# A retention layer and two dense layers in one program: the opening written as a table of single-engine steps

## The chip, the core and the metric

The kernel runs on one core of a Trainium2 chip. The metric is the time of one execution in device microseconds; the time of a version is the median of its runs. TensorE (PE in the views) multiplies matrices, with its weight loads shown apart as PEld; VectorE is DVE, ScalarE is ACT, GpSimd is POOL, and SyncE (SP) issues most of the transfers.

## What is computed

```python
# q, k, v: (2, 8, 768, 64); w_in: (512, 2048), w_out: (2048, 512), twice
gamma = 1.0 - 2.0 ** (-5.0 - arange(8))
for t in range(768):
    state = gamma * state + outer(k[t], v[t])     # per batch and head
    y[t] = q[t] @ state / sqrt(64)
x = y as (1536 tokens, 512)
h = x @ w_in1;  x = where(h > 0, h, exp(min(h, 0)) - 1) @ w_out1
h = x @ w_in2;  x = (max(h, 0) + log1p(exp(-abs(h)))) @ w_out2
```

q, k and v are float32. The four weights arrive as 8-byte numbers, from which the kernel rebuilds a float32 on the chip.

## The kernel before

**Retention.** The 1536 tokens are twelve tiles of 128, six for each batch entry. For tile j, q and k are transposed on TensorE (`ret_transpose`, L194); the transposed q is evacuated from PSUM by DVE, which multiplies it with the table gq of decays (L209), and the transposed k by ACT (L207). `ret_scores` (L236) multiplies the two and DVE applies the causal mask (L248). `ret_out` (L252) multiplies the state (where there is one) and the masked scores with the tokens' values; the result is a column block of the activations x, kept as a rounded high part xh (ACT, L272) and a low part xl (DVE, L273). `ret_state` (L218) carries the state to the next tile, `ret_wide` spreads it on POOL (L216), and `ret_prep` decays v on POOL (L192).

**The dense layers.** Four tiles make a block of 512 tokens; there are three blocks. A unit u is one of two layers, one of three blocks and one of sixteen slices of 128 hidden features, 96 units in all. `hidden(u)` (L297) is twelve matmuls of 128x512: the slice's high and low weights against xh and xl, three products by four parts of the depth. `act(u)` applies the activation, `act_split` splits its result into gh and gl (L326, L327), `project(u)` (L347) is twelve matmuls into four accumulators, and `finish` writes a finished block.

**Weights.** A weight slice arrives in a raw buffer (five of them, `load_w`, L129). `conv_w` rebuilds it: two operations on ACT (L143, L144), then two on DVE (L145, L146). `split_w` makes the high part wh on ACT (L157) and the low part wl on DVE (L158). The order of the slices is in `wq`; the next one is loaded when a buffer has been converted. From block 0 of the first layer 32 slices are converted, and 32 more for the second layer in block 2.

**What sets the order.** The schedule is manual: each engine takes its instructions in the order in which the program issues them, with semaphores between engines, and the order is that of the calls. The opening is written out (L393 to L425): `next_load(5)`, then `load_tile(4)`, then the four tiles with scores, output of the tile before, transposes of the next, state. From unit 0 on the loop at L438 issues for every u the split of u+3, the splits for u+1, `hidden(u+2)`, one conversion, one retention job of tiles 4 to 11 (transposes, scores, or output with state, L370), `project(u)`, `act(u+2)` and one or two conversions more. All loads of tiles and weights are on SP's queue, in this order; a load into a buffer still in use holds the queue. PSUM has eight banks: before unit 0 the retention rotates over seven, then over r0 and r1, while hidden uses h0 and h1 and project a0 to a3. `keep_clock(7)` (L107) runs seven matmuls on zeros ahead of the first transpose.

```python
    for s in range(TPB):
        ret_scores(s)
        ...
        if s:
            ret_out(s - 1)
        if s + 1 < TPB:
            ret_transpose(s + 1)
        ret_state(s)
```

Of the kernel before, what the change touches and what calls it, by code (L numbers as in the profile page):

```python
# [23 lines left out]
def tile_retention_elu_softplus(
# [43 lines left out]
    def load_tile(j):  # L68
        b, c = divmod(j, CPB)
        r = []  # L70
        for n, (src, nm) in enumerate(((q, "q"), (k, "k"), (v, "v"))):
            if j == 0 and n == 2:
                nc.sync.dma_start(out=gq, in_=decay_q)
            t = early[n][:, j] if j < TPB else rp.tile([P, H, D], F32, tag=nm, name=nm)
            nc.sync.dma_start(out=t, in_=src[b, :, c * P:(c + 1) * P, :].rearrange("h s d -> s h d"))
            r.append(t)
        qkv[j] = r
# [71 lines left out]
    free = {(0, f, o) for f in range(NF) for o in range(2)}  # L149

    def split_w(u, o):
        _, _, f = units[u]
        a = wf[f][o]
        sh = [P, DM] if o else [P, KK, P]
        h = wsp.tile(sh, F32R, tag=f"wh{o}", name="wh")
        l = wsp.tile(sh, F32R, tag=f"wl{o}", name="wl")
        nc.scalar.activation(out=h, in_=a, func=AF.Copy)  # L157
        nc.vector.tensor_tensor(out=l, in0=a, in1=h.bitcast(F32), op=ALU.subtract)  # L158
        ws[u, o] = (h, l)
        if units[u][:2] == (0, NB - 1):  # L160
            free.add((1, f, o))
# [334 lines left out]
```

## Time and profile before

| | |
|---|---|
| runs, us | 598.36, 598.55, 596.74 (median 598.36) |
| the profiled execution, us | 598.43 |
| its span, us | 596.7 |
| PE busy | 584.9 us, 98% |
| DVE busy | 463.9 us, 78% |
| ACT busy | 415.3 us, 70% |
| POOL busy | 24.9 us, 4% |
| mean granted clock of TensorE | 0.992 |

The span runs from the first to the last instruction of the profiled execution; its time has some two microseconds more around that. A granted clock of 1.00 is 2.4 GHz, 0.50 is 1.2 GHz. PE's busy share says little of how well it is used, since matmuls overlap; where it is idle, in what stretch and for whom, is read from the stretches, the timeline and the chain of waits.

### The profile page before, as it was taken

The page shows a single profiled execution, that of the slowest core. Times are in us where ns is not written, and L with a number is a line of the kernel's source. Part 1 is how long each engine was busy: PE and PEld are TensorE (multiplying, and loading weights), DVE is VectorE, ACT ScalarE, POOL GpSimd, SP SyncE. Part 2 cuts the span into 40 slices and gives each one's busy share as a digit, 9 for nine tenths or more (in the row PEclk, how much of TensorE's full clock was granted, in tenths as well). Part 3 has the DMA queues.
Part 4 walks back from the last instruction along what each step waited for, and adds up shares of the span by engine and source line. Part 5 has one row for each costly group of instructions (what it writes and reads, how often), then busy time and mean ns, then how long its engine had stood idle before and what let it go on. Part 6 is the DMA issues. An engine that isn't in the chain of part 4 may idle for free.

```text
span 596.7 us, 8178 instructions
## 1 busy us (share of the span) xinstructions
PE 584.9 (98%) x3031; PEld 482.0 (81%) x3031; DVE 463.9 (78%) x741; ACT 415.3 (70%) x699; POOL 24.9 (4%) x42
## 2 busy tenths in 40 slices
PE   8898999999999999999999999999999999999997
PEld 5776888888888888888888888888888888888885
DVE  3889999965655455898898999877877787878774
ACT  2499788844544465898898967776777667766763
POOL 3300200111011000000000000000000000000000
PEclk8998999999999999999999999999999999999999
DMA  9986776851010000355464000000100000100001
GB/s 200 285 238 211 196 209 197 211 127 35 18 36 2 1 0 8 99 177 164 156 206 145 1 1 1 1 0 1 71 1 1 0 1 0 71 1 2 0 1 71
DMA packets 61000, 46.94 MB, mean 79 GB/s; under 512 B 38816, under 2 KB 55200, under 8 KB 60960
## 3 DMA queue, kind: packets, MB, share of 16 engines
q1 hardware_dynamic: 60672, 46.14, 27.5%
q8 instruction: 24, 0.39, 0.3%
q10 hardware_dynamic: 288, 0.27, 0.1%
q14 instruction: 16, 0.13, 0.1%
HBM read 43.26 MB, written 3.15 MB: 78 GB/s over the span
## 4 chain that ended last, share of the span: by engine, by line
PE 95%; DVE 2%; ACT 1%; DMA 1%; issue 1%; SPq 0%; DVEq 0%; ACTq 0%
PE h L297 42%; PE a L347 37%; PE r L347 7%; PE r L241 2%; PE r L267 1%; PE r L200 1%; PE r L261 1%; DMA gq<-decay_q 1%; DVE cl L145 1%; PE r L225 0%; PE a L200 0%; PE a L241 0%; DVE wi L146 0%; PE h L241 0%; DVE wo L146 0%
## 5 line engine op out<-in xcount | busy, mean ns | idle before, releaser
L297 PE MATMUL h<-xh,wh 128*128 128x512 f32 x384 | 103.0, 390 | 1.8 <-ACT wh L157 1.0
L297 PE MATMUL h<-xh,wl 128*128 128x512 f32 x384 | 102.7, 389 | 0.0
L297 PE MATMUL h<-xl,wh 128*128 128x512 f32 x384 | 102.7, 389 | 0.0
L297 PEld LDWEIGHTS h<-xh,wh 128*128 128x128 f32 x384 | 71.8, 188 | 17.7 <-ACT wh L157 2.0
L297 PEld LDWEIGHTS h<-xh,wl 128*128 128x128 f32 x384 | 72.1, 188 | 15.0
L297 PEld LDWEIGHTS h<-xl,wh 128*128 128x128 f32 x384 | 72.1, 188 | 15.0
L157 ACT ACTIVATE wh<-wo 128x512 fp32r<-128x512 f32 x96 | 60.4, 629 | 34.0 <-PE a L347 30.5
L158 DVE TENSOR_TENSOR wl<-wo,wh 128x512 fp32r<-128x512 f32 x96 | 67.3, 701 | 15.3 <-ACT wh L157 15.2
L158 DVE TENSOR_TENSOR wl<-wi,wh 128x512 fp32r<-128x512 f32 x96 | 65.7, 685 | 0.1
L157 ACT ACTIVATE wh<-wi 128x512 fp32r<-128x512 f32 x96 | 59.5, 619 | 1.6 <-DVE wi L146 1.5
L347 PE MATMUL a<-gh,wh 128*128 128x512 f32 x192 | 57.8, 408 | 0.0
L347 PE MATMUL a<-gh,wl 128*128 128x512 f32 x192 | 54.4, 390 | 0.0
L347 PE MATMUL a<-gl,wh 128*128 128x512 f32 x192 | 54.3, 389 | 0.0
L145 DVE SCALAR_TENSOR_TENSOR cl<-cm,cl 128x512 int32<-128x512 int32 x64 | 46.0, 719 | 10.2 <-ACT cl L144 10.0
L326 ACT ACTIVATE gh<-w 128x512 fp32r<-128x512 f32 x48 | 30.4, 633 | 33.1 <-DVE w L318 33.1
L312 ACT ACTIVATE e<-h 128x512 f32<-128x512 f32 x48 | 28.6, 597 | 32.0 <-PE h L297 32.0
L315 DVE TENSOR_SCALAR w<-e 128x512 f32<-128x512 f32 x48 | 20.5, 426 | 36.9 <-ACT e L313 36.7
L144 ACT ACTIVATE cl<-raw,half 128x512 int32<-128x512 uint32 x64 | 48.0, 750 | 0.0
L307 DVE SCALAR_TENSOR_TENSOR e<-e,h 128x512 f32<-128x512 f32 x48 | 32.8, 683 | 16.2 <-ACT e L306 15.9
L347 PEld LDWEIGHTS a<-gh,wl 128*128 128x128 f32 x192 | 36.2, 188 | 7.8
L143 ACT ACTIVATE cm<-raw 128x512 f32<-128x512 f32 x64 | 42.2, 659 | 0.0
L347 PEld LDWEIGHTS a<-gl,wh 128*128 128x128 f32 x192 | 36.0, 188 | 7.6
(114 smaller groups left out, 904.0 us busy)
## 6 DMA issues: line engine op xcount, KB each, us to landing
raw<-moe_w_in SPq DMA_DIRECT2D x32, 512.0 KB, 4.0
raw<-moe_w_out SPq DMA_DIRECT2D x32, 512.0 KB, 3.4
out_dram<-o SPq DMA_DIRECT2D x11, 256.0 KB, 2.1
q<-q SPq DMA_DIRECT2D x8, 256.0 KB, 4.5
k<-k SPq DMA_DIRECT2D x8, 256.0 KB, 5.0
v<-v SPq DMA_DIRECT2D x8, 256.0 KB, 5.4
xl<-q SPq DMA_DIRECT2D x4, 256.0 KB, 5.2
xh<-k SPq DMA_DIRECT2D x4, 256.0 KB, 5.2
```

Source lines behind the costliest of these rows:

```text
L143: nc.scalar.activation(out=m, in_=hi.bitcast(F32), func=AF.Copy, scale=2.0 ** -112)
L144: nc.scalar.activation(out=l, in_=lo.bitcast(U32), func=AF.Relu, scale=2.0 ** -29, bias=half)
L145: nc.vector.scalar_tensor_tensor(out=l, in0=m.bitcast(I32), scalar=3, in1=l, op0=ALU.logical_shift_left, op1=ALU.bitwise_or)
L157: nc.scalar.activation(out=h, in_=a, func=AF.Copy)
L158: nc.vector.tensor_tensor(out=l, in0=a, in1=h.bitcast(F32), op=ALU.subtract)
L241: nc.tensor.matmul(bs[i][:, pr * P:(pr + 1) * P], kT[i * D:(i + 1) * D, pr, :], qT[i * D:(i + 1) * D, pr, :], start=(pr == 0), stop=(pr == ...
L297: nc.tensor.matmul(b, w[:, kk, :], x[:, kk, :], start=(n == 0), stop=(n == len(seq) - 1))
L307: nc.vector.scalar_tensor_tensor(out=e, in0=e, scalar=-1.0, in1=h, op0=ALU.add, op1=ALU.max)
L312: nc.scalar.activation(out=e, in_=h, func=AF.Abs)
L315: nc.vector.tensor_scalar(out=w, in0=e, scalar1=1.0, scalar2=-1.0, op0=ALU.add, op1=ALU.add)
L326: nc.scalar.activation(out=gh, in_=g, func=AF.Copy)
L347: nc.tensor.matmul(acc[i], st[:, i * P:(i + 1) * P], mv, start=(f == 0 and p == 0), stop=(f == NF - 1 and p == 2))
```

## The change

The program's calls are cut into steps that each concern one engine (and SP for loads), a dictionary gives each a short name, and the program is now a list of names with a number, `name.j`. Of the names: `Lq Lk Lv Lg Lw` load q, k, v of a tile, gq, and entry j of the weight list; `dq` and `dv` decay q and v; `Tq Tk` transpose on TensorE and `tq tk` evacuate; `S` scores and `m` masks; `O` outputs, `xh xl` their parts; `ST st` the state, `sp` its spreading; `ca cb` the halves of a conversion on ACT and DVE; `ih il oh ol` the splits of w_in and w_out; `H` hidden, `aa ab` the activation's parts, `gh gl` its split, `R` project, `F` finish; `kc` clock-keeping matmuls.

`regular()` generates a list in the manner of the old program. The 244 steps of the table `OPENING`, up to the sixth projection, are issued first, in the table's order; the rest of the generated list follows. Tiles 0 and 1 (those with a `dq` step) have q multiplied by its decay in place, on DVE, ahead of the transpose, and their evacuation is a copy; the table of decays grows from 12 to 20 columns for that. `keep_clock` is called for five matmuls more. `project` opens the accumulators at the first unit of a block that is issued (`fresh`), which in the table is unit 1. In the generated list a conversion's ACT half comes ahead of its DVE half with other steps between.

```diff
+OPENING = """
+Lq.0 Lk.1 Lk.0 Lq.1 dq.0 Lv.0 Tq.0 kc.3 Lk.2 Lq.2 Tk.0 kc.2 Lv.1 Tk.1 dq.1 tk.1 Lg.0 tq.0 Tq.1 Lv.2 tk.0 dv.0 tq.1 S.0
+Lk.3 ST.0 Lq.3 m.0 Lv.3 Tq.2 Tk.2 Lk.4 S.1 tk.2 dv.1 Lw.0 Lw.1 tq.2 Lw.2 ST.1 st.0 Lq.4 O.0 m.1 dv.2 Lw.3 S.2 Lq.5
...
-    def conv_w(layer, f, o):
-        if (layer, f, o) not in raws:
+    def conv_a(i):
+        if i not in raws:
...
+        nc.scalar.activation(out=m, in_=r[:, :, :, 1].bitcast(F32), func=AF.Copy, scale=2.0 ** -112)
+        nc.scalar.activation(out=l, in_=r[:, :, :, 0].bitcast(U32), func=AF.Relu, scale=2.0 ** -29, bias=half)
+        parts[i] = (m, l)
+
+    def conv_b(i):
...
+        m, l = parts.pop(i)
...
         nc.vector.scalar_tensor_tensor(out=l, in0=m.bitcast(I32), scalar=3, in1=l, op0=ALU.logical_shift_left, op1=ALU.bitwise_or)
...
+    def decay_query(j):
+        nc.vector.tensor_tensor(out=qkv[0, j], in0=qkv[0, j], in1=gt, op=ALU.mult)
...
+        if n:
+            nc.scalar.activation(out=tf, in_=b, func=AF.Copy)
+        elif j in plain:
+            nc.vector.tensor_copy(tf, b)
+        else:
+            nc.vector.tensor_tensor(out=tf, in0=b, in1=gq, op=ALU.mult)
...
-        if f == 0:
+        fresh = (layer, blk) not in opened
+        if fresh:
+            opened.add((layer, blk))
...
-    for u in range(NU):
-        layer, blk, f = units[u]
-        if u + LOOK + 1 < NU:
-            split_w(u + LOOK + 1, 0)
...
+        for u in range(NU):
+            cb()
+            if u + 3 < NU:
+                add("ih il", u + 3)
...
+            ca()
+            if u + 1 < NU:
+                add("oh ol gh gl", u + 1)
...
+            if u + 2 < NU:
+                add("H", u + 2)
+            cb()
+            if jobs:
+                names, j = jobs.pop(0)
...
+    opening = OPENING.split()
+    plain = {int(t[3:]) for t in opening if t[:3] == "dq."}
+    seen = set(opening)
+    rest = regular()
...
+    for t in opening + [t for t in rest if t not in seen]:
+        name, j = t.split(".")
+        steps[name](int(j))
```

**SP's queue at the start.** The early q, k and v lie in the tiles named xl_88, xh_89 and xl_90; raw is a weight's buffer. Before:

```order
L75 DMA xl_88<-q 128x8x64
L75 DMA xh_89<-k 128x8x64
L73 DMA gq<-decay_q 128x512
L75 DMA xl_90<-v 128x8x64
L75 DMA xl_88<-q 128x8x64
L75 DMA xh_89<-k 128x8x64
L75 DMA xl_90<-v 128x8x64
L75 DMA xl_88<-q 128x8x64
L75 DMA xh_89<-k 128x8x64
L75 DMA xl_90<-v 128x8x64
L75 DMA xl_88<-q 128x8x64
L75 DMA xh_89<-k 128x8x64
```

Now:

```order
L85 DMA xl_88<-q 128x8x64
L85 DMA xh_89<-k 128x8x64 x2
L85 DMA xl_88<-q 128x8x64
L85 DMA xl_90<-v 128x8x64
L85 DMA xh_89<-k 128x8x64
L85 DMA xl_88<-q 128x8x64
L85 DMA xl_90<-v 128x8x64
L414 DMA gq<-decay_q 128x512
L85 DMA xl_90<-v 128x8x64
L85 DMA xh_89<-k 128x8x64
L85 DMA xl_88<-q 128x8x64
L85 DMA xl_90<-v 128x8x64
```

k of tile 1 and k of tile 0 (in this order, one row for both) stand second and third, gq has gone from the third place to the ninth, behind v of tile 1, and v of tile 0 behind q of tile 1.

**TensorE around the first hidden matmuls.** The rows at the shape 128x128 and 64x128 are retention (L261, L267 outputs; then L295, L301 outputs, L222 transposes, L273 scores). Before, from the output of tile 3 to unit 2:

```order
L261 MATMUL a_409<-xh_91,wide_159 128x128 x4
L267 MATMUL a_409<-A,xl_90 64x128 x8
L297 MATMUL h_434<-xh_258,wh 128x512 x4
L297 MATMUL h_434<-xh_258,wl 128x512 x4
L297 MATMUL h_434<-xl_259,wh 128x512 x4
L297 MATMUL h_463<-xh_258,wh 128x512 x4
L297 MATMUL h_463<-xl_259,wh 128x512 x4
L297 MATMUL h_463<-xh_258,wl 128x512 x4
L297 MATMUL h_524<-xh_258,wh 128x512 x4
L297 MATMUL h_524<-xl_259,wh 128x512 x4
L297 MATMUL h_524<-xh_258,wl 128x512 x4
```

Now, over the same stretch up to the output of tile 4; of the eight score rows of tile 4 the first two are shown, and unit 1's three rows are left out:

```order
L295 MATMUL a_403<-xh_91,wide_146 128x128 x4
L301 MATMUL a_403<-A,xl_90 64x128 x8
L222 MATMUL a_425<-ident,k 128x128 x4
L222 MATMUL a_432<-ident,q 128x128 x4
L329 MATMUL h_448<-xh_293,wh 128x512 x4
L329 MATMUL h_448<-xh_293,wl 128x512 x4
L329 MATMUL h_448<-xl_294,wh 128x512 x4
L273 MATMUL r_475<-qT,kT 128x128
L273 MATMUL r_476<-qT,kT 128x128
L222 MATMUL r_516<-ident,q 128x128 x4
L295 MATMUL r_526<-qT,wide_145 128x128 x4
L301 MATMUL r_526<-A,v 64x128 x8
```

Tile 4's transposes stand ahead of unit 0, its scores behind unit 0, and the query transposes of tile 5 and tile 4's output behind unit 1, all ahead of unit 2; before, the hidden matmuls of units 0, 1 and 2 followed one another.

**DVE around tile 4's query.** cl and wi or wo are the two operations of a conversion, wl and gl low parts, qT the evacuation of a transposed query, L283 (L248 before) a mask. Before, the twelve rows up to tile 4's query:

```order
L146 SCALAR_TENSOR_TENSOR wi_134<-raw,cl 128x512
L307 SCALAR_TENSOR_TENSOR e<-e,h_524 128x512
L145 SCALAR_TENSOR_TENSOR cl<-cm,cl 128x512
L146 SCALAR_TENSOR_TENSOR wo_131<-raw,cl 128x512
L145 SCALAR_TENSOR_TENSOR cl<-cm,cl 128x512
L146 SCALAR_TENSOR_TENSOR wi_136<-raw,cl 128x512
L158 TENSOR_TENSOR wl<-wi_134,wh 128x512
L158 TENSOR_TENSOR wl<-wo_131,wh 128x512
L327 TENSOR_TENSOR gl<-e,gh 128x512
L145 SCALAR_TENSOR_TENSOR cl<-cm,cl 128x512
L146 SCALAR_TENSOR_TENSOR wo_133<-raw,cl 128x512
L209 TENSOR_TENSOR qT<-r_614,gq 128x512
```

Now, from the first conversion to the first mask of tile 4:

```order
L165 SCALAR_TENSOR_TENSOR cl<-cm,cl 128x512
L166 SCALAR_TENSOR_TENSOR wi_113<-raw,cl 128x512
L165 SCALAR_TENSOR_TENSOR cl<-cm,cl 128x512
L166 SCALAR_TENSOR_TENSOR wi_115<-raw,cl 128x512
L312 TENSOR_TENSOR xl_294<-h_378,xh_293 128x4x128
L179 TENSOR_TENSOR wl<-wi_113,wh 128x512
L312 TENSOR_TENSOR xl_294<-a_403,xh_293 128x4x128
L237 TENSOR_TENSOR qT<-a_432,gq 128x512
L179 TENSOR_TENSOR wl<-wi_115,wh 128x512
L165 SCALAR_TENSOR_TENSOR cl<-cm,cl 128x512
L166 SCALAR_TENSOR_TENSOR wi_117<-raw,cl 128x512
L283 TENSOR_TENSOR A<-r_475,mask 128x512
```

The evacuation of tile 4's query stands behind two conversions, two tiles' low parts and unit 0's; before, ten conversions went ahead of it.

## Rows read from the trace of the kernel before

**Rows 1.** The page, part 4: the chain that ended last, shares by engine.
```profile
PE 95%; DVE 2%; ACT 1%; DMA 1%; issue 1%; SPq 0%; DVEq 0%; ACTq 0%
```

**Rows 2.** Stretches, us: each engine's busy time, granted clock, DMA share, GB/s.
```profile
0.00:28.00 28.00, 23.48 (x256) 18.12 (x257) 15.53 (x27) 9.18 (x14) 9.66 (x22) 0.94 1.11 243
28.00:57.00 29.00, 26.00 (x120) 20.73 (x120) 26.55 (x43) 26.81 (x47) 1.34 (x2) 0.94 0.79 229
57.00:120.00 63.00, 63.00 (x390) 51.99 (x389) 59.41 (x94) 52.23 (x92) 5.04 (x7) 1.00 0.73 204
```

**Rows 3.** Timeline of TensorE, opening: start us, us, instruction, idle before and releaser.
```profile
1.26 3.00 PE L107 MATMUL wb<-warm 128*128 128x512 bf16 x7 [1.26 <-DVE warm L102]
4.14 0.63 PE L200 MATMUL h<-ident,xl 128*128 128x128 f32 x4
...
6.97 1.75 PE L241 MATMUL a<-qT,kT 64*128 64x128 f32 x16 [1.06 <-DVE qT L209]
...
27.73 1.20 PE L297 MATMUL h<-xh,wh 128*128 128x512 f32 x4 [0.70 <-ACT xh L272]
...
34.48 1.17 PE L297 MATMUL h<-xh,wh 128*128 128x512 f32 x4 [0.99 <-ACT wh L157]
...
51.57 1.96 PE L241 MATMUL r<-qT,kT 64*128 64x128 f32 x16 [1.87 <-DVE qT L209]
53.46 1.95 PE L347 MATMUL a<-gh,wh 128*128 128x512 f32 x4
55.26 1.07 PE L347 MATMUL a<-gh,wl 128*128 128x512 f32 x4
...
57.07 1.07 PE L297 MATMUL h<-xh,wh 128*128 128x512 f32 x4
```

**Rows 4.** The chain that ended last in order of time: start us, us, work.
```profile
1.93 4.11 DMA gq<-decay_q
...
16.96 1.09 PE h L261 x8
18.05 1.02 PE h L267 x16
19.07 1.02 PE a L200 x8
20.10 0.64 PE a L225 x16
...
71.63 2.72 PE h L297 x12
74.35 1.09 PE r L241 x16
...
214.30 2.72 PE a L347 x12
```

**Rows 5.** DMA issues: line's tile, queue, operation, count, KB each, median us to landing.
```profile
xl<-q SPq DMA_DIRECT2D x4, 256.0 KB, 5.2
...
dec<-decay ACTq DMA_DIRECT2D x1, 6.0 KB, 2.6
```

**Rows 6.** Timeline, opening, of SP's queue and of POOL.
```profile
5.81 0.94 SPq L75 DMA_DIRECT2D xl<-v  x1
...
7.37 1.05 POOL L192 TENSOR_TENSOR xl<-xl,dec 128x512 f32<-128x512 f32 x1 [4.78 <-DMA xl<-v]
...
22.89 1.04 POOL L192 TENSOR_TENSOR xl<-xl,dec 128x512 f32<-128x512 f32 x1
```

**Rows 7.** Timeline of DVE, conversions and splits.
```profile
23.55 0.93 DVE L145 SCALAR_TENSOR_TENSOR cl<-cm,cl 128x512 int32<-128x512 int32 x1
...
58.19 0.68 DVE L145 SCALAR_TENSOR_TENSOR cl<-cm,cl 128x512 int32<-128x512 int32 x1
...
59.52 0.69 DVE L158 TENSOR_TENSOR wl<-wi,wh 128x512 fp32r<-128x512 f32 x1
60.12 0.69 DVE L158 TENSOR_TENSOR wl<-wo,wh 128x512 fp32r<-128x512 f32 x1
```

More of the change, by code (lines that the diff above doesn't have):

```diff
@@ L66, in tile_retention_elu_softplus, with load @@
     qkv = {}
-    def load_tile(j):
+    def load(n, j):
         b, c = divmod(j, CPB)
[L70 to L77, printed above, removed]
+        src, nm = ((q, "q"), (k, "k"), (v, "v"))[n]
+        t = early[n][:, j] if j < TPB else rp.tile([P, H, D], F32, tag=nm, name=nm)
+        nc.sync.dma_start(out=t, in_=src[b, :, c * P:(c + 1) * P, :].rearrange("h s d -> s h d"))
+        qkv[n, j] = t
     early = [xpool.tile([P, TPB, H, D], F32, tag=t, name=t) for t in ("xl2", "xh2", "xl1")]
     early_t = xpool.tile([P, 4, HP, P], F32, tag="xh1", name="xh1")
-    dec = const.tile([P, H + HP], F32, name="dec")
+    dec = const.tile([P, 2 * H + HP], F32, name="dec")
     gq = const.tile([P, HP * P], F32, name="gq")
     nc.scalar.dma_start(out=dec, in_=decay)
-    for j in range(TPB):
-        load_tile(j)
     gv = dec[:, 0:H].unsqueeze(2).to_broadcast([P, H, D])
+    gt = dec[:, H + HP:].unsqueeze(2).to_broadcast([P, H, D])
     gs = dec[:, H:H + HP].unsqueeze(2).to_broadcast([P, HP, D])
@@ L148, in tile_retention_elu_softplus, with split_h, split_l @@
     ws = {}
-    free = {(0, f, o) for f in range(NF) for o in range(2)}
-    def split_w(u, o):
+    def split_h(o, u):
         _, _, f = units[u]
[L153 to L161, printed above, removed]
+        h = wsp.tile([P, DM] if o else [P, KK, P], F32R, tag=f"wh{o}", name="wh")
+        nc.scalar.activation(out=h, in_=wf[f][o], func=AF.Copy)
+        ws[u, o] = [h]
+    def split_l(o, u):
+        _, _, f = units[u]
+        l = wsp.tile([P, DM] if o else [P, KK, P], F32R, tag=f"wl{o}", name="wl")
+        nc.vector.tensor_tensor(out=l, in0=wf[f][o], in1=ws[u, o][0].bitcast(F32), op=ALU.subtract)
+        ws[u, o].append(l)
     slots = {}
@@ L287, in tile_retention_elu_softplus @@
     acc = {}
+    opened = set()
     def hidden(u):
@@ L314, in act, with act_b @@
             nc.scalar.activation(out=l, in_=e, func=AF.Ln, bias=one)
+            acts[u] = [e, l]
+    def act_b(u):
+        h = hb.pop(u)
+        e = acts[u][0]
+        if units[u][0] == 0:
+            nc.vector.scalar_tensor_tensor(out=e, in0=e, scalar=-1.0, in1=h, op0=ALU.add, op1=ALU.max)
+        else:
+            l = acts[u][1]
+            w = rp.tile([P, TB], F32, tag="qT", name="w")
             nc.vector.tensor_scalar(out=w, in0=e, scalar1=1.0, scalar2=-1.0, op0=ALU.add, op1=ALU.add)
@@ L346, in project @@
             st, mv = passes[p]
-            nc.tensor.matmul(acc[i], st[:, i * P:(i + 1) * P], mv, start=(f == 0 and p == 0), stop=(f == NF - 1 and p == 2))
+            nc.tensor.matmul(acc[i], st[:, i * P:(i + 1) * P], mv, start=(fresh and p == 0), stop=(f == NF - 1 and p == 2))
     def finish(u):
@@ L381, in next_load @@
-    def next_load(n):
-        for _ in range(n):
-            x = next(lw, None)
-            if x:
-                load_w(*x)
-    def next_conv(n):
-        for _ in range(n):
-            if cv and cv[0] in free:
-                conv_w(*cv.pop(0))
-                next_load(1)
-    next_load(5)
-    load_tile(4)
-    cv = list(wq)
-    ret_transpose(0)
-    ret_prep(0)
-    for s in range(TPB):
-        ret_scores(s)
-        if s == TPB - 1:
-            next_conv(1)
-        if s:
-            ret_out(s - 1)
-        if s + 1 < TPB:
-            ret_transpose(s + 1)
-        ret_state(s)
-        ret_wide(s + 1)
-        ret_prep(s + 1)
```

345 lines of the change are left out of this document (212 added, 133 removed).

## The prediction

> **What bounds the kernel now.** I read the page first: TensorE is on the chain that ended last for 95% of the span [rows 1], so only time that TensorE loses can be won. The stretches [rows 2] tell where it loses any: it is busy 63.00 of 63.00 us from 57 to 120 us (and goes on so to the last matmuls), but 23.48 of 28.00 before 28 us, and 26.00 of 29.00 from 28 to 57 us. The same rows show VectorE (DVE) at 26.55 of 29.00 and ScalarE (ACT) at 26.81 of 29.00 in the second stretch: there the weights' conversion and splitting fills both, and TensorE waits for them. In the third stretch DVE has 59.41 of 63.00, so it keeps up, barely.
>
> TensorE's own rows [rows 3] show the losses singly: 1.06 us for the first decayed query (whose multiplication waits for the table gq), 0.70 for the last tokens, 0.99 for the third split weight, 1.87 for tile 4's query. The last is the dearest, because the clock falls with it: tile 4's scores take 1.96 us and the first quarter of the next projection 1.95, where the same work takes 1.09 [rows 4] and, in that projection's next row, 1.07 [rows 3]. The first scores also ran slowly: 1.75 us.
>
> **What TensorE loses before.** T, S, O and ST are a tile's transposes, scores, outputs and state; H and R a unit's hidden and projection matmuls. At full clock they take 1.02 (T), 1.09 (S), 1.09 + 1.02 (O; 1.02 alone for tile 0, which has no state), 0.64 (ST), 2.72 (H) and 2.72 (R) [rows 4]. From the first transpose at 4.14 to the start of H.5 at 57.07 [rows 3] TensorE does T.0 to T.4 (5.10), S.0 to S.4 (5.45), O.0 to O.3 (1.02 + 3 x 2.11 = 7.35), ST.0 to ST.3 (2.56), H.0 to H.4 (13.60) and R.0 to R.2 (8.16): 42.2 us of work in 52.9. Lost: 10.7 us.
>
> **The change, part by part.**
>
> *The first loads.* On SP's queue k of tile 1 now stands second, k of tile 0 third, q of tile 1 fourth, q of tile 2 seventh, gq ninth. By place: the third issue of before (gq) landed 4.11 us after 1.93 [rows 4], so at 6.0; the fourth (v of tile 0) was in use at 7.37 [rows 6]. So k of tile 0 lands at 6.0 and q of tile 1 by 7.4. Later ones land 5.2 us after issue [rows 5]: q of tile 2 in the place issued at 5.81 [rows 6], at 11.0.
>
> *Query decay of tiles 0 and 1 ahead of the transpose (dq).* gq is no longer needed first; instead DVE multiplies q in place before T. That needs the table dec, which landed 2.6 us after its issue in the first microsecond [rows 5], and q of tile 0, on hand by 4.14. No such multiplication stands on DVE's rows; the nearest, a tensor-tensor with both inputs in SBUF, takes 0.69 [rows 7], the far end is POOL's product of the same shape with dec, 1.05 [rows 6]. I take 0.69, of the same engine: T of q.0 starts at 4.85 instead of 4.14, 0.71 lost (1.07 at the far end). For tile 1 it ends at 7.37 + 0.69 = 8.06; then tile 0's transposed query is evacuated, until 8.75 (a copy now, which I cost like a split, 0.69). S.0 starts at 8.9, where it started at 6.97. Both T.0 and T.1 are done by then: the 4.05 us from 4.85 hold 2.04 of work, 2.0 lost. The five added clock-keeping matmuls lie in these waits (for k.0 and q.1) and cost nothing; without that cover they would cost 5 x 3.00/7 = 2.1 [rows 3]. Whether S.0 still runs slowly (1.75 for 1.09) the rows leave open: between 0 and 0.66 lost. I take 0.66, since gaps remain ahead of it.
>
> *Tiles 1 to 3.* ST.0 ends by 11.2, about when q of tile 2 lands; I take 0.45 lost for a late q here or at tile 3. gq, two places on, is issued near 8 and lands near 13, and is first needed for S.2, which now comes behind S.1, ST.1 and O.0, at 15. The other waits of before are covered, since a tile's transposes stand well ahead of its scores. Lost in all: 0.71 + 2.0 + 0.66 + 0.45 = 3.8.
>
> *Tile 4 moved up.* T.4 fills the time in which H.0 waited 0.70 for tokens; S.4 stands between H.0 and H.1, O.4 before H.2, T.5 and ST.4 around H.2 and H.3: work that came later stands where the 0.99 was. Tile 4's query is evacuated on DVE ahead of the third conversion, so the 1.87 and the slow 1.7 behind it have no cause left. On SP, k.4 goes ahead of the first weight, which comes a place (some 0.9 us, as the 0.94 of [rows 6]) later; ACT is not free for it before tile 1's tokens, near 20. v.4 goes behind weight load 4, which waits until the first conversion frees its buffer: issued near 25, landed by 31, decayed on POOL by 32; O.4 comes at 34.4.
>
> *Conversions in halves.* The instructions are the same, ACT's half sooner. DVE is what can fail. A conversion takes 1.33 there, a split 0.61, start to start [rows 7]. With H.0 at 27.3 by the sum so far, DVE starts the first conversion at 23.4, behind tile 3's masks. Up to the low split of unit 3 it does six conversions (8.0), 0.5 extra for two beside POOL, eleven operations of 0.61 (6.7) and a short wait for S.4: done at 39.0, where H.3 wants it at 41. The low split of unit 4 follows at 49.4 (H.4 wants it at 50.3), gl of unit 1 comes at 42.7 (R.1 wants it at 43.5), gl of unit 3 at 55 (R.3 wants it at 56.9). DVE holds with 0.9 us to spare at the tightest.
>
> The 0.5 stands for this: the conversion's first operation took 0.93 instead of 0.68 while POOL ran its product [rows 7]. The Trainium skill's "SBUF — State Buffer", section "SBUF: two separate sides", has the port pair of these two engines as an exclusive lock: the loser waits out the other's whole instruction. By that rule each of the two meetings could cost up to POOL's 1.04, 2.1 for the 0.5; the 0.9 to spare would be gone and TensorE lose 0.7, 592.2 for the sum below. The row shows a quarter of that, so the sum keeps the row.
>
> *Later.* From unit 12 on as many conversions stand ahead of each H as before, and tiles 5 to 11 come three units sooner on an engine that is never idle there: no cost. Done before H.5 beyond the old list are R.3, T.5, S.5, O.4 and ST.4: 2.72 + 1.02 + 1.09 + 2.11 + 0.64 = 7.6. H.5 then starts at 4.14 + 3.8 + 42.2 + 7.6 = 57.7, 0.7 late with 7.6 done: a gain of 6.9, which is also 10.7 - 3.8. The profiled execution took 598.43 (span 596.7), 0.07 over the median of 598.36. **598.4 - 6.9 = 591.5 us.** If the clock holds and q.2 lands in time, 2.7 are lost and it is 590.4; if q.1 is on hand with k.0 at 6.0 too, S.0 comes 1.4 sooner: 589.0.
>
> **Rivals.** *DVE comes late.* Between 28 and 57 us it idled 29.00 - 26.55 = 2.45 us before. If that idling stays, R.1 or H.4 waits 2.45 - 0.9 = 1.6, and such a wait cost a fallen clock of 0.87 + 0.88 = 1.7 last time: 3.3 given back, 594.8. For it: its 94% up to 120 us. Against: ACT's halves, which it depends on, now lead. *TensorE's clock stays low.* Rows 3 show slow scores behind a gap of 1.06. If the gaps before S.0 and at tiles 2 and 3 keep it down until H.0, the 16.2 us of T, S, O and ST after S.0 grow by the 1.75 / 1.09 of S.0's row: +9.8, and 591.5 + 9.8 = 601.3, **slower**. It decides if tiles 1 to 3 each bring a gap of about a microsecond; against it, their rows at 16.96 to 20.10 [rows 4] stood at full clock although gaps went before them. *The waits only change places.* If loads and evacuations come late enough for TensorE to lose the 10.7 again, the time is 598.4; little speaks for it, since most of its waits were for DVE, whose order is what the table changes.
>
> **How the numbers follow.** Same means within 0.3%, 1.8 us, about what a measurement of this kernel can tell. Chances: forecast 0.72 (589 to 593.5), DVE late 0.18, places only 0.05, clock low 0.05. Faster by more than 0.3% (below 596.6) are the first and nearly all of the second, 0.89; same 0.06; slower 0.05. The range 589.0 to 596.0 takes in the forecast with its bounds and the DVE case with 1.2 us more, and leaves out the rest.
>
> **What would show it.** Right: S.0 near 9, H.0 near 27, H.5 near 57.7 with tile 5's scores done; no wait of TensorE over 0.7 us from 11 us on, and its granted clock full from 12 us. Wrong: a wait of TensorE for a low split (wl) or gl between 40 and 57 us (DVE late), slow scores after 15 us (clock), any wait behind 57 us, or H.5's start with less than 7 us of extra work done.

## The result and the profile after

| | before | changed |
|---|---|---|
| runs, us | 596.59 to 598.55, median 597.55 (4) | 591.32 to 592.34, median 591.74 (4) |
| the profiled execution, us (its span) | 598.43 (596.7) | 591.32 (589.4) |
| PE, DVE, ACT busy, us | 584.9, 463.9, 415.3 | 582.7, 464.4, 414.6 |

The ratio is **0.9903, 95% interval [0.988, 0.9927]**: faster, 5.8 us of 597.55. The forecast was 591.5 with a range of 589.0 to 596.0. The forecast gain of 6.9 was counted from one execution of 598.43; the 18 runs of before beside e1, e2b, e10 and e11 lie in two groups, twelve of 596.7 to 597.3 with a mean granted clock of 0.998 to 1.0 (one of 0.996) and six of 598.2 to 598.6 with 0.994 to 0.996, and that execution (0.992) lies with the second, though the clock is not the whole account, since a run of 598.0 beside e9 and one of 598.3 beside e3 had 1.0.

The stretches of the changed kernel (each engine's busy time, granted clock, DMA share, GB/s), against [rows 2]:

```profile
0.00:28.00 28.00, 25.96 (x279) 20.19 (x280) 19.26 (x34) 11.77 (x19) 9.55 (x22) 1.00 1.00 267
28.00:57.00 29.00, 29.00 (x181) 23.62 (x180) 27.98 (x44) 25.27 (x44) 5.04 (x5) 1.00 0.75 224
57.00:120.00 63.00, 63.00 (x396) 52.02 (x396) 60.61 (x96) 53.00 (x92) 5.34 (x6) 1.00 0.70 210
120.00:585.00 465.00, 464.77 (x2188) 384.71 (x2184) 356.52 (x572) 324.12 (x545) 6.46 (x9) 1.00 0.13 41
```

TensorE is busy 25.96 of 28.00 us (23.48 before) and 29.00 of 29.00 (26.00), at full clock throughout (0.94 in both before): 5.5 us of idle time have gone. DVE has 27.98 of 29.00 (26.55). All that TensorE waited for in the whole span, by the view of its waits (total, times, longest, us; the first stands before too, while the zeros are made):

```profile
PE wb L115 <- DVE warm L110: 1.3, 1, 1.3
PE a L273 <- ACT kT L233: 0.4, 1, 0.4
PE h L222 <- DVE xl L214: 0.2, 1, 0.2
```

TensorE's timeline at the places of [rows 3], the columns as there:

```profile
4.62 0.63 PE L222 MATMUL h<-ident,xl 128*128 128x128 f32 x4 [0.23 <-DVE xl L214]
...
8.61 0.37 PE L273 MATMUL a<-qT,kT 64*128 64x128 f32 x1 [0.42 <-ACT kT L233]
...
25.53 1.17 PE L329 MATMUL h<-xh,wh 128*128 128x512 f32 x4
...
28.47 1.16 PE L273 MATMUL r<-qT,kT 64*128 64x128 f32 x16
...
34.87 1.20 PE L329 MATMUL h<-xh,wh 128*128 128x512 f32 x4
...
49.97 1.16 PE L273 MATMUL r<-qT,kT 64*128 64x128 f32 x16
...
56.64 1.07 PE L329 MATMUL h<-xh,wh 128*128 128x512 f32 x4
```

The first transpose comes 0.48 later than before (4.62 for 4.14), the first scores at 8.61 (6.97 before). Then nothing is late: unit 0 starts at 25.53 without the 0.70, unit 2 at 34.87 without the 0.99, tile 5's scores at 49.97 take 1.16 where tile 4's took 1.96 behind a wait of 1.87. H.5 starts at 56.64 instead of 57.07, with T.5, S.5, O.4, ST.4 and R.3 done besides.

### The profile page after: what moved, and what is told of

Same layout as the page of the kernel before. It is cut to its first block, busy times and chain, and to the rows that moved or that the text cites. A ratio compares the mean times of both kernels' runs of the same rounds, so it can differ in the third digit from the quotient of the medians.

```text
span 589.4 us, 8211 instructions
## 1 busy us (share of the span) xinstructions
PE 582.7 (99%) x3036; PEld 480.5 (82%) x3036; DVE 464.4 (79%) x743; ACT 414.6 (70%) x699; POOL 26.4 (4%) x42
## 4 chain that ended last, share of the span: by engine, by line
PE 95%; DVE 2%; ACT 1%; issue 1%; DMA 1%; DVEq 0%; ACTq 0%
PE h L329 43%; PE a L391 36%; PE r L391 7%; PE r L273 2%; PE r L301 2%; PE r L295 1%; PE r L222 1%; PE r L253 1%; DMA xl<-q 1%; PE a L222 0%; PE h L222 0%; PE a L273 0%; PE a L301 0%; PE a L295 0%; DVE cl L165 0%
## 5 line engine op out<-in xcount | busy, mean ns | idle before, releaser
L391 PE MATMUL a<-gh,wh 128*128 128x512 f32 x192 | 56.5, 401 | 0.0
L343 ACT ACTIVATE e<-h 128x512 f32<-128x512 f32 x48 | 28.6, 596 | 32.1 <-PE h L329 32.1
L338 ACT ACTIVATE e<-h 128x512 f32<-128x512 f32 x48 | 28.6, 595 | 27.8 <-PE h L329 26.8
```

The lines of the kernel that those rows point to most:

```text
L338: nc.scalar.activation(out=e, in_=h, func=AF.Relu, scale=-1.0)
L343: nc.scalar.activation(out=e, in_=h, func=AF.Abs)
L391: nc.tensor.matmul(acc[i], st[:, i * P:(i + 1) * P], mv, start=(fresh and p == 0), stop=(f == NF - 1 and p == 2))
```

## The experiments

Each has its own runs of before beside it on its chip; the last column compares the ratios, times 597.5 us, so by the two intervals together it is good to 1.5 to 1.8 us.

| run | what | median, us | ratio to before, 95% | against the changed kernel, us |
|---|---|---|---|---|
| e9 | before + first part | 595.58 | 0.9963 [0.9948, 0.9978] | +3.6 |
| e8 | before + tile 4 moved up | 599.12 | 1.0019 [1.0006, 1.0032] | +6.9 |
| e11 | before + ACT's halves sooner | 596.69 | 0.9993 [0.9983, 1.0003] | +5.4 |
| e1 | changed, generated list alone | 598.82 | 1.0026 [1.0013, 1.0038] | +7.3 |
| e2 | changed, tile 4 later | 598.32 | 1.0009 [0.9995, 1.0023] | +6.3 |
| e2b | the same, its low parts placed better | 595.09 | 0.9965 [0.9951, 0.9978] | +3.7 |
| e5 | changed, halves glued | 599.90 | 1.0036 [1.0021, 1.0051] | +7.9 |
| e3 | changed, no early decay | 591.86 | 0.9900 [0.9885, 0.9915] | -0.2 |
| e4 | changed, no added clock-keeping matmuls | 591.81 | 0.9903 [0.9884, 0.9921] | 0.0 |
| e6 | changed, two additions on DVE | 592.46 | 0.9913 [0.9898, 0.9927] | +0.6 |
| e7 | changed, six additions on DVE | 595.58 | 0.9961 [0.9945, 0.9976] | +3.5 |
| e10 | changed, first copies sooner | 591.55 | 0.9905 [0.9891, 0.9918] | +0.1 |

### One part alone, in the kernel before

**e9: the first loads, the early decay and the clock-keeping matmuls.**

```diff
-    for j in range(TPB):
-        load_tile(j)
+    for n, j in ((0, 0), (1, 1), (1, 0), (0, 1), (2, 0), (1, 2), (0, 2), (2, 1)):
+        load_tile(j, (n,))
+    nc.sync.dma_start(out=gq, in_=decay_q)
...
+    def ret_decay(j):
+        nc.vector.tensor_tensor(out=qkv[j][0], in0=qkv[j][0], in1=gt, op=ALU.mult)
```

> The kernel before the change with the other part: loads in the new order, q of tiles 0 and 1 decayed ahead of the transpose, five clock-keeping matmuls, both tiles' transposes ahead of the first scores; the rest as before. My theory: the first scores start near 8.6 us at full clock and end near 9.7, where scores and tile 1's transposes ended at 10.7 before: 1.0 us gained there, unit 0's hidden matmuls 1 to 1.5 us earlier, and the waits of 0.70, 0.99 and 1.87 us stay: 1.0 us faster (0.5 to 2). Rival (what follows hangs on DVE and the conversions, so an earlier start of the retention is lost again before unit 3): within 0.5 us of before, with longer waits of TensorE at units 0 to 3.

2.2 us faster than before by the ratio. In its timeline TensorE has

```profile
26.67 1.20 PE L308 MATMUL h<-xh,wh 128*128 128x512 f32 x4 [0.70 <-ACT xh L283]
...
33.15 1.17 PE L308 MATMUL h<-xh,wh 128*128 128x512 f32 x4 [0.71 <-ACT wh L159]
...
50.20 1.16 PE L252 MATMUL r<-qT,kT 64*128 64x128 f32 x16 [1.86 <-DVE qT L220]
```

Unit 0 starts 1.06 sooner (27.73 in [rows 3]); the wait of unit 2 is 0.71 for 0.99. Tile 4's scores still wait 1.86 for their query, but take 1.16: the clock did not fall, while behind the 1.87 of [rows 3] it did. At like clocks (0.998 to 1.0) five runs of e9 take 595.2 to 595.6 where the runs of before beside it take 596.6 to 597.2 (nine; a tenth took 598.0): about 1.4 us are the part's own, within what was expected. The rest of the 3.0 between the two profiled executions (595.4 and 598.43) is about what the clock's fall behind the 1.87 cost, 1.7.

**e8: tile 4's retention among the first units, with its loads one place earlier.**

```diff
+    ret_transpose(4)
     hidden(0)
+    ret_scores(4)
     next_conv(2)
     hidden(1)
+    ret_end(4)
...
-    for j in range(TPB, NTILE):
+    for j in range(TPB + 1, NTILE):
```

> The kernel before the change with one part of it: tile 4 moved up (transposes before unit 0's hidden matmuls, scores behind them, output and state behind unit 1's), and the later tiles' jobs one tile earlier; no table, no halves, no new loads. My theory: the waits of 0.70, 0.99 and 1.87 us and the slow 1.7 us behind the last shrink or go, while DVE gets 3.3 us of tile 4's work in its fullest stretch: 3 us faster than before (between 1.5 and 4.7), with tile 4's scores at full clock. Rival (DVE is the limit in that stretch, so its added work pushes the splits back as far as TensorE is filled): less than 1 us faster.

It gains nothing and is 1.1 us slower, as the rival had it, but not only for the rival's reason: two of the new waits are for loads. The timeline shows the waits in new places:

```profile
27.59 0.63 PE L200 MATMUL r<-ident,q 128*128 128x128 f32 x4 [0.98 <-DMA q<-q]
...
28.67 0.63 PE L200 MATMUL r<-ident,k 128*128 128x128 f32 x4 [0.45 <-DMA k<-k]
...
40.97 1.47 PE L297 MATMUL h<-xh,wh 128*128 128x512 f32 x4 [2.51 <-ACT wh L157]
...
58.38 1.16 PE L241 MATMUL r<-qT,kT 64*128 64x128 f32 x16 [1.02 <-DVE qT L209]
```

Tile 4's q and k are not there when its transposes come (0.98 and 0.45), unit 2's weight is 2.51 late, and tile 5's query 1.02.

**e11: only the order of the halves.**

```diff
-            if cv and cv[0] in free:
-                conv_w(*cv.pop(0))
+            if not begun:
+                begin()
+            if begun:
+                conv_b(*begun.pop(0))
...
+            begin()
```

where `begin` issues ACT's half of the next conversion and `conv_b` DVE's half.

> The kernel before with one part of the change alone: the scalar engine's half of each weight conversion is issued one conversion ahead of the vector engine's half, all else in the old order. Theory (the vector engine stops waiting for the scalar engine's half, which is worth something only where a weight is late): the waits of the units 2 and 5 shrink by part of a microsecond each, 0.5 to 2 us faster than before. Rival (the tensor engine is bound by the query's tiles there, not by the halves): within 0.3 us of the kernel before. Rival (holding a second raw buffer delays the loads): up to 2 us slower.

0.4 us by the ratio, an interval that includes no change: between theory and rival, too near to both to tell. Its timeline shows what became of the waits:

```profile
35.29 1.16 PE L306 MATMUL h<-xh,wh 128*128 128x512 f32 x4 [1.72 <-DVE e L316]
...
51.45 1.16 PE L250 MATMUL r<-qT,kT 64*128 64x128 f32 x16 [0.89 <-ACT e L315]
```

The 0.99 and the 1.87 of [rows 3] have become 1.72 (for DVE's activation) and 0.89: 2.6 in place of 2.9. Alone, the three parts give 2.2, -1.1 and 0.4 us, 1.5 in all, where the whole change gives 5.8.

### One part taken out of the changed kernel

**e1: the table emptied.** The generated list orders everything; early decay, tile 4 moved up and separate halves remain.

```diff
 OPENING = """
-Lq.0 Lk.1 Lk.0 Lq.1 dq.0 Lv.0 Tq.0 kc.3 Lk.2 Lq.2 Tk.0 kc.2 Lv.1 Tk.1 dq.1 tk.1 Lg.0 tq.0 Tq.1 Lv.2 tk.0 dv.0 tq.1 S.0
...
+
 """
```

> The table is left empty; the generated list of steps (tile 4 up at its own place, the halves at their fixed distance, query decay in natural layout for tiles 0 and 1) orders the whole program. Theory (the gain hangs on where each half and each load stands, and the table sets that for the first stretch): the waits for late weights come back in the first hidden units, 2 to 6 us: 594 to 598, nearer the kernel before than the changed one. Rival (splitting and moving up is enough, any order does): within 1 us of the changed kernel, 590.8 to 592.8. Rival (without the table the list is worse than the old loops): over 598.5.

At 598.82 the last rival was right: without the table the list is worse than the old loops. TensorE's waits over 1 us from 10 us on, from its timeline:

```profile
10.36 0.66 PE L212 MATMUL r<-ident,xl 128*128 128x128 f32 x4 [1.43 <-DVE xl L204]
...
28.70 1.19 PE L319 MATMUL h<-xh,wh 128*128 128x512 f32 x4 [1.17 <-ACT xh L297]
...
36.92 1.17 PE L319 MATMUL h<-xh,wh 128*128 128x512 f32 x4 [1.16 <-DVE e L342]
...
50.05 0.80 PE L212 MATMUL r<-ident,q 128*128 128x128 f32 x4 [2.00 <-DVE xl L302]
```

They are for the decay of tile 1's query, the last tokens, the activation and the low part of tile 4's tokens, each a DVE or ACT step that stands too far back in a queue; behind the last the granted clock is 0.61 and 0.54 for 4 us. **In this order the same steps gain nothing, so the gain hangs on the order.** It is one other order, not all.

**e2 and e2b: tile 4 back in tile 5's places of the table.**

```diff
-sp.4 ca.1 cb.0 O.3 xh.2 cb.1 Lw.4 ih.0 Lv.4 Tk.4 xh.3 xl.2 Tq.4 Lw.7 ih.1 il.0 Lq.7 tk.4 xl.3 H.0 few.0 ca.2 tq.4 il.1
+sp.4 ca.1 cb.0 O.3 xh.2 cb.1 Lw.4 ih.0 Lv.4 xh.3 xl.2 Lw.7 ih.1 il.0 xl.3 H.0 few.0 ca.2 il.1 ca.3 cb.2 aa.0 H.1 Lw.6
...
+cb.11 cb.10 ca.12 H.5 Lw.15 ih.6 cb.12 Lw.16 oh.4 ca.13 ol.4 Tk.5 ab.4 O.4 ST.4 tk.5 xh.4 xl.4 st.4 sp.5 dv.5 Lq.6
```

> The changed kernel with its table, but tile 4 not moved up: tile 4 takes tile 5's places in the table, tile 5 tile 6's, and the later tiles come one job later, as before the change. My theory (tile 4's transposes, scores and output fill TensorE's waits around units 0 to 2): waits come back before unit 0 (about 0.7 us, for tile 3's tokens), before unit 2 (about 0.7, for its high split) and before the first projection (about 0.4, for the low parts): 1.7 us slower than the changed kernel, up to 3.5 if the clock falls with one of them. Rival (the order of the conversions and splits alone brings the gain, the filling none): under 0.5 us slower, no wait of TensorE over 0.3 us between 24 and 45 us.

It lost 6.3, too much for either. The gaps at the start came as expected, but I had put tile 4's low part too far ahead: DVE idled 2.96 us for an output that TensorE gave later, and TensorE, up to 67 us, waited 2.0 and 1.9 us for what stood behind it in DVE's queue. The run doesn't measure what tile 4's place is worth. In e2b its parts stand behind unit 7:

```diff
-cb.11 cb.10 ca.12 H.5 Lw.15 ih.6 cb.12 Lw.16 oh.4 ca.13 ol.4 Tk.5 ab.4 O.4 ST.4 tk.5 xh.4 xl.4 st.4 sp.5 dv.5 Lq.6
...
+cb.14 aa.5 gh.4 Lw.20 ab.5 ca.15 Tq.5 tq.5 oh.5 il.7 H.7 xh.4 gh.5 xl.4 ST.4 st.4 sp.5 dv.5 ih.8 gl.4 R.4 cb.15 aa.6
```

> Tile 4 again in tile 5's places of the table, but this time its copies stand where tile 5's stood (behind unit 7's first result) and its state is updated behind them, so that the vector engine no longer idles on tile 4's output; everything else as in the changed kernel. Theory (tile 4 between units 0 and 3 is worth what it covers there): without it the tensor engine again waits about 0.7 us before unit 0, 0.5 us of work less covers the start and 1.4 us pass before unit 2, as in the earlier run of this pair, and the 3.9 us that this run lost at 59 to 67 us are gone: 2 to 3 us slower than the changed kernel, 593.5 to 595. Rival (the delay at 59 to 67 us comes from having any fifth tile's work there at all): again about 598. Rival (the early gaps are taken back later): within 0.5 us of the changed kernel, under 592.4.

3.7 us slower (3.4 by the medians). On TensorE's timeline:

```profile
26.33 1.19 PE L328 MATMUL h<-xh,wh 128*128 128x512 f32 x4 [0.70 <-ACT xh L306]
...
33.94 1.19 PE L328 MATMUL h<-xh,wh 128*128 128x512 f32 x4 [1.43 <-ACT wh L172]
```

These are the waits of [rows 3] again, 0.70 for 0.70 and 1.43 for 0.99, 2.1 together, and no other wait of TensorE's from unit 0 on is longer than 0.2. The profiled execution loses 3.9 against the changed kernel's; a further 1.0 of it lies ahead of the first scores, which start at 9.62 in this execution (below, e6). What tile 4's place is worth is thus 2.1 by the waits and 3.7 by the ratio: the theory's 2 to 3, or a little more.

**e5: each ACT half issued directly ahead of its DVE half.**

```diff
-    for t in opening + [t for t in rest if t not in seen]:
+    glued = []
+    for t in opening + [t for t in rest if t not in seen]:
+        if t[:3] == "cb.":
+            glued.append("ca" + t[2:])
+        if t[:3] != "ca.":
+            glued.append(t)
+    for t in glued:
```

> The changed kernel with each conversion's ACT half moved to directly ahead of its DVE half, through the whole program; nothing else. My theory (the halves apart spare DVE its waits for ACT in the full stretch): DVE waits about 0.5 us before a conversion in places, 2 us in all between 23 and 57 us, more than the 0.9 us it has to spare, so TensorE waits 1 us or more between 30 and 57 us: 1 to 3.4 us slower than the changed kernel (with or without a fall of the clock). Rival (DVE's waits are made up elsewhere): within 0.5 us, no wait of TensorE over 0.3 us.

More than twice the upper end of what was expected. The stretch from 28 to 57 us:

```profile
28.00:57.00 29.00, 25.62 (x161) 19.56 (x159) 21.81 (x35) 19.87 (x34) 3.56 (x4) 1.00 0.69 200
```

DVE and ACT are both *less* busy than in the changed kernel (21.81 for 27.98, 19.87 for 25.27), because they wait for each other. DVE's timeline, then ACT's:

```profile
45.93 0.69 DVE L165 SCALAR_TENSOR_TENSOR cl<-cm,cl 128x512 int32<-128x512 int32 x1 [1.41 <-ACT cl L153]
...
55.13 0.94 DVE L165 SCALAR_TENSOR_TENSOR cl<-cm,cl 128x512 int32<-128x512 int32 x1 [1.29 <-ACT cl L153]
```

```profile
57.62 0.63 ACT L173 ACTIVATE wh<-wo 128x512 fp32r<-128x512 f32 x1 [2.00 <-DVE wo L166]
```

Five conversions on DVE in this stretch stand 0.7 to 2.0 us for the ACT half issued just before them, and ACT's splits wait for DVE's results. TensorE waits 2.20 and 1.87 for low parts of weights. In this table the distance between the halves is what keeps both engines at work.

**e3: no early decay; gq third on SP's queue again.**

```diff
-Lq.0 Lk.1 Lk.0 Lq.1 dq.0 Lv.0 Tq.0 kc.3 Lk.2 Lq.2 Tk.0 kc.2 Lv.1 Tk.1 dq.1 tk.1 Lg.0 tq.0 Tq.1 Lv.2 tk.0 dv.0 tq.1 S.0
+Lq.0 Lk.1 Lk.0 Lg.0 Lq.1 Lv.0 Tq.0 kc.3 Lk.2 Lq.2 Tk.0 kc.2 Lv.1 Tk.1 tk.1 tq.0 Tq.1 Lv.2 tk.0 dv.0 tq.1 S.0 Lk.3 ST.0
```

> The changed kernel without the decay of q ahead of the transposes of tiles 0 and 1: their queries are multiplied with gq at the evacuation, as before, and gq is loaded third again, so that k of tile 0 and all later loads come a place later. My theory: the load order matters more than where the product stands; k of tile 0 lands about 0.9 us later, the first scores start near 9.2 instead of 8.6 us: 0.6 us slower than the changed kernel, up to 1.7 if the clock falls before them. Rival (the early decay is the main gain of the opening): 2 us or more slower.

No difference that the runs can tell, so neither the theory nor the rival held: the first scores start at 8.76 (8.61 with it), not near 9.2. This execution began at the slower of two speeds of the opening (below): its first four transposes, from 4.22 on, took 1.06.

**e4: the `kc` steps do nothing** (the five added matmuls; the seven at the start stay).

```diff
-             "kc": keep_clock,
+             "kc": lambda n: None,
```

> The changed kernel without any of its twelve clock-keeping matmuls. Theory: without work before 9 us TensorE's clock is at its lower level when the retention begins and stays so into it; scores, transposes and outputs of tiles 0 and 1 (5 us at full clock) take 1.6 times as long: 1 to 3 us slower than the changed kernel, with a granted clock of 0.5 in part of the stretch before 15 us. Rival (the retention's own matmuls bring the clock up soon enough, and loads set the pace before 9 us): within 0.5 us; the five matmuls between the transposes even lie in the way of tile 1's and it is 0.5 us faster.

No difference either, and the granted clock is given as 1.00 all the same, although TensorE had 0.6, 0.5 and 0.3 us of waits in the first 11 us. The rival was right. The first four transposes took 1.08 here, but so they did in executions with the added matmuls (1.09 in e6's and e10's).

### The spare time of DVE, and a candidate

**e6 and e7: two and six additions of 128x512 on DVE behind tile 4's masks.**

```diff
+    def spare(n):
+        for _ in range(n):
+            nc.vector.tensor_tensor(out=idle, in0=idle, in1=idle, op=ALU.add)
...
-ca.3 cb.2 S.4 aa.0 H.1 m.4 Lw.6 Lk.5 cb.3 ca.4 ab.0 Tq.5 Lw.9 Lv.5 dv.4 O.4 aa.1 cb.4 ih.2 ca.5 il.2 H.2 ab.1 ih.3
+ca.3 cb.2 S.4 aa.0 H.1 m.4 xx.2 Lw.6 Lk.5 cb.3 ca.4 ab.0 Tq.5 Lw.9 Lv.5 dv.4 O.4 aa.1 cb.4 ih.2 ca.5 il.2 H.2 ab.1
```

> The changed kernel with two useless additions of 128x512 (0.61 us each) on DVE behind tile 4's masks, near 31 us: DVE is 1.2 us later from there on. My theory (DVE has about 0.9 us to spare, at the first projection's low part of the activation and at unit 4's low split): TensorE waits about 0.3 us, 0.2 to 0.5 us slower than the changed kernel. Rival (DVE has no time to spare): 1.2 us slower. Rival (it has several us): nothing, and no wait of TensorE.

> The same with six additions, 3.7 us of DVE. My theory (0.9 us to spare): TensorE waits 2.8 us between 36 and 50 us, in one or two pieces, and the clock may fall with it for 1.7 us more: 2.8 to 4.5 us slower than the changed kernel, shown as waits before the projection of unit 1 and unit 4's third pass. Rival (no time to spare): 3.7 or more. Rival (several us to spare): under 1 us.

The additions take longer than the 0.61 each that was expected. Each reads what the one before wrote, and starts 0.72 behind it, as the second operation of a conversion does behind the first: the two of e6 hold DVE for 1.32, the six of e7 for 4.23 (from 31.24 to the next conversion at 35.47). The conversion behind them no longer meets POOL's product, which saves 0.30. Counted from tile 4's masks, DVE is 0.97 later at gl of unit 1 in e6 and 3.94 later at unit 0's activation in e7.

In e6 the view lists no wait of TensorE's matmuls between 28 and 57 us, but its weight load for the first projection's gl waits, where the theory had it. DVE in e6, then TensorE at the first matmul of that projection and the first on gl, in the changed kernel and in e6 (there the weight load of that matmul):

```profile
42.51 0.68 DVE L376 TENSOR_TENSOR gl<-e,gh 128x512 fp32r<-128x512 f32 x1
```

```profile
41.59 0.50 PE L391 MATMUL a<-gh,wh 128*128 128x512 f32 x1
...
42.16 0.39 PE L391 MATMUL a<-gl,wh 128*128 128x512 f32 x1
```

```profile
42.53 0.50 PE L398 MATMUL a<-gh,wh 128*128 128x512 f32 x1
...
43.24 0.19 PEld L398 LDWEIGHTS a<-gl,wh 128*128 128x128 f32 x1 [0.41 <-DVE gl L376]
```

gl ends at 43.19 and is taken at 43.24, 0.71 behind the projection's start instead of 0.57, and from that start to H.4 pass 5.84 instead of 5.57: 0.27 lost, the theory's 0.3. In e7 the wait stands elsewhere than expected, ahead of unit 2's hidden matmuls, for the activation of unit 0:

```profile
31.24 4.32 DVE L210 TENSOR_TENSOR idle<-idle 128x512 f32<-128x512 f32 x6
```

```profile
37.62 1.58 PE L336 MATMUL h<-xh,wh 128*128 128x512 f32 x4 [2.31 <-DVE e L359]
```

2.31 of 3.94 come through, so DVE had 1.6 to spare here; in the changed kernel's trace it is 1.70, from the end of this row at 33.17 to unit 2 at 34.87:

```profile
32.49 0.68 DVE L352 SCALAR_TENSOR_TENSOR e<-e,h 128x512 f32<-128x512 f32 x1
```

Behind the wait of 2.31 the granted clock is 0.54 and 0.60 for 4 us. That is the rival "DVE comes late" of the prediction, brought about by hand, with its fallen clock, 3.5 us in all. Of e6's 0.6 the additions thus explain 0.27. Its profiled execution, 1.25 longer than the changed kernel's, lost 0.94 more ahead of H.0, before the edit acts, with slower first matmuls. Its timeline, to compare with 4.62 and 8.61 above:

```profile
4.66 1.09 PE L229 MATMUL h<-ident,xl 128*128 128x128 f32 x4 [0.23 <-DVE xl L221]
...
5.54 1.49 PE L115 MATMUL wb<-warm 128*128 128x512 bf16 x3
...
9.68 0.37 PE L280 MATMUL a<-qT,kT 64*128 64x128 f32 x1 [0.74 <-ACT kT L240]
```

The same transposes take 1.09 for 0.63, and the first scores come 1.07 later. e2b's profiled execution began like this too.

**e10: tile 0's copies moved ahead**, so that the first scores need not wait 0.42.

```diff
-Lq.0 Lk.1 Lk.0 Lq.1 dq.0 Lv.0 Tq.0 kc.3 Lk.2 Lq.2 Tk.0 kc.2 Lv.1 Tk.1 dq.1 tk.1 Lg.0 tq.0 Tq.1 Lv.2 tk.0 dv.0 tq.1 S.0
+Lq.0 Lk.1 Lk.0 Lq.1 dq.0 Lv.0 Tq.0 tq.0 kc.3 Lk.2 Lq.2 Tk.0 tk.0 kc.2 Lv.1 Tk.1 dq.1 tk.1 Lg.0 Tq.1 Lv.2 dv.0 tq.1 S.0
```

> The changed kernel with two entries of the table moved up: tile 0's copies of the transposed key and query directly behind their own transposes, so that the first scores need not wait 0.42 us for the scalar engine's copy of the key. Theory (the first hidden unit's start is set by the conversion of the first weights, whose load lands about 20.1 us, and not by the scores; the runs without the early decay and without the clock-keeping matmuls moved the first scores by 0.2 us and the time not at all): within 0.3 us of the changed kernel. Rival (every tenth that the tensor engine starts earlier is kept, since it is busy from the first scores on): 0.2 to 0.5 us faster, 591.2 to 591.5.

The time can't tell theory from rival (591.55 lies 0.2 under the changed kernel's median, by the ratio it is 0.1 over). The 0.42 is gone; in this execution another wait stands in its place, for q of tile 2, and unit 0 starts at 25.75 (25.53 in the changed kernel).

```profile
10.70 0.63 PE L222 MATMUL h<-ident,xl 128*128 128x128 f32 x4 [0.46 <-DMA xl<-q]
```

TensorE has no idle time worth naming behind this in either kernel, so its start is not set by the landing of the first weight, as the theory had it; here a wait taken away came back at the next load. No version here is faster than the changed kernel beyond the noise; e3 and e4 are as fast with less in them.

## Why the prediction held, and where it did not

**The place of the loss** was right: TensorE's idle time up to 57 us, and no other (after 120 us it idles 0.23 of 465, where before idled nothing). The table removes nearly all of it, and in e1, e2b and e5 waits come back.

**Lost up to H.5**: predicted 3.8, measured at the same prices 56.64 - 4.14 - (42.2 + 7.6) = 2.7. That is the case the prediction priced at 590.4. Two terms failed: the slow first scores (0.66) didn't come, since they ran at full clock, and the 0.45 for a late q of tile 2 didn't either. The latter is real all the same: e4's and e10's executions have just that wait, 0.46 each. 0.71 + 2.0 up to the first scores were 2.4 (8.61 for 8.9); within it the 0.71 for the early decay is 0.48 by the first transpose, and e3's first scores come no sooner without it. The last wait ahead of them is for ACT's copy of the key, 0.42 and in e3 0.50.

Behind the first scores TensorE waits for nothing, and the remaining 0.3 is two wrong prices: the retention up to H.0 took 0.4 less than its prices, and from H.0 to H.5 TensorE took 0.7 more, because a unit's twelve matmuls take 2.72 only between other units; next to retention work they take 2.8 to 2.9 (34.87 to 37.72, for one). That H.0 came at 25.53, where it was predicted near 27, is the two terms, the 0.3 up to the first scores and the first of these prices.

**The work done ahead of H.5** was priced too high: 7.6 at the prices of the opening. From H.5 to the end the program takes 589.4 - 56.64 = 532.8 where it took 596.7 - 57.07 = 539.6, so it was worth 6.9. Of the 0.7 missing, 0.23 is idle time that has come in behind 120 us; the rest, 0.5, lies in what the steps cost before at their later places, and wasn't split further. So H.5's start and the work were off by 1.1 and 0.7 in opposite directions: that 591.5 came within 0.2 of 591.32 is partly luck.

**The baseline**: the prediction counted 2.4 of the 10.7 lost as the clock's (0.66 and 1.7) and overlooked 1.06 more: tile 1's transposes, right behind the slow scores, took 2.08 (8.66 to 10.74) for 1.02, at a granted clock of 0.50. In before:

```profile
8.66 1.11 PE L200 MATMUL a<-ident,xl 128*128 128x128 f32 x4
```

Not all of these 3.4 are to be won by a full clock: in e8's execution, with the first loads of before, scores and transposes ran at full speed, but tile 1's transposes waited 0.38 and 0.57 for q and k. The other executions of before don't all have these falls, by their mean granted clocks. The predicted time is for that reason better than the predicted gain: 6.9, against 5.8 by the ratio.

**DVE's spare time**: predicted 0.9, at gl of unit 1 and the low split of unit 4. In the changed kernel's trace of DVE they are

```profile
40.61 0.69 DVE L369 TENSOR_TENSOR gl<-e,gh 128x512 fp32r<-128x512 f32 x1
...
47.23 0.68 DVE L179 TENSOR_TENSOR wl<-wi,wh 128x512 fp32r<-128x512 f32 x1
```

ended at 41.30 and 47.91, where TensorE takes them at 42.16 and 48.98: 0.86 and 1.07 to spare. e6 confirms size and place: 0.97 later at gl of unit 1 costs 0.27. The rival of 594.8 is some three conversions of 1.33 away: e7, 3.94 later, took 595.58.

**The added clock-keeping matmuls** cost nothing, as predicted. That they were of use was not said, and e4 shows no use beyond the noise.

**The parts**: the prediction summed them as if each had its own worth. The runs contradict that: tile 4 moved up is worth 2 to 4 us in the table and less than nothing in the old order; separate halves are worth 7.9 there and 0.4 alone. In these runs a part by itself mostly moves a wait.

**The weighing of the lock** failed in its reading. The row at 23.55 [rows 7] began when POOL's product [rows 6] had run 0.66 of its 1.04; its 0.93 is not "a quarter" but the remaining 0.38, and then 0.55 of its own. The rows of the changed kernel, POOL's and then DVE's, say the same:

```profile
30.26 1.04 POOL L217 TENSOR_TENSOR v<-v,dec 128x512 f32<-128x512 f32 x1 [7.37 <-DMA v<-v]
...
84.50 1.36 POOL L217 TENSOR_TENSOR v<-v,dec 128x512 f32<-128x512 f32 x1
```

```profile
30.86 0.98 DVE L165 SCALAR_TENSOR_TENSOR cl<-cm,cl 128x512 int32<-128x512 int32 x1
...
84.89 1.53 DVE L179 TENSOR_TENSOR wl<-wi,wh 128x512 fp32r<-128x512 f32 x1
```

POOL ends at 31.30 and 85.86; DVE ends 0.54 and 0.56 later, so an operation of 0.68 becomes 0.98 or 1.53 according to when it meets the other. POOL's own 1.36 fits the same from the other side: a DVE operation ran from 84.19 to 84.96 when it began. The Trainium skill's "SBUF — State Buffer", section "SBUF: two separate sides", has the loser waiting out the other engine's whole instruction: the traces agree. That the sum was not hurt (the rule's 592.2 against 591.74) has another cause: the two meetings with POOL's products between 28 and 57 us (at 30.86, and at 51.14 another of 1.53) cost 0.30 and 0.85, not 2.1. The first is paid already where gl of unit 1 has its 0.86 to spare, the second comes behind both tight places, and TensorE waits for neither.

## What to carry to other kernels

When several engines share a pipeline, ask of each part of a reordering what it does alone and what it does with the other queues as they are: here no part was worth more than 2.2 us alone, and the whole 5.8. In a full schedule, try issuing a producer's half a whole step ahead of its consumer's half; back to back, both engines idled here for each other although neither had more to do. Count a loss that comes from a fallen clock apart from the wait in front of it, and look whether every execution has it, before taking one execution as the baseline.
